# Another hand-fixed order of the same 573 steps in a two-part state-space kernel on one core

## The chip, the core and the metric

The kernel runs on one core of a Trainium2 chip. The metric is the device time of one execution in microseconds (us), lower is better. Five engines work side by side, each through its own instructions in a fixed order: PE (TensorE, matmuls), DVE (VectorE), ACT (ScalarE), POOL (GpSimd) and SP (SyncE, which here issues nearly all DMA transfers). [...] The time before is 198.16 us, the median of three runs (197.69 to 199.36).

## What is computed

Two independent parts, written side by side into one output of 2048 rows by 1280 columns.

```python
def _A_ref(x, Lambda_re, Lambda_im, B_re, B_im, C_re, C_im, log_dt, Dskip):   # S5
    Lam_bar = jnp.exp(dt * Lam)
    Bu = jnp.einsum("bld,pd->blp", x + 0j, B_bar)
    for t in range(L):
        h = Lam_bar[None, :] * h + Bu[:, t, :]
    y = 2.0 * jnp.einsum("blp,dp->bld", hseq, Cmat).real + x * Dskip[None, None, :]
...
def _B_ref(q, k, v, shift_k, ssm_k, ssm_D):                                    # H3
    k_shift = k_shift + k_pad[:, t:t + S, :] * shift_k[:, ks - 1 - t][None, None, :]
    kv = k_shift * v
    y = irfft(rfft(kv) * rfft(ssm_k))[:S]  +  kv * ssm_D
    return q * y
...
return jnp.concatenate([a, b], axis=-1)     # L = S = 2048, D = P = 640, 4 taps
```

The second part is cut here to its steps: the transform runs over the 2048 rows, zero-padded to 4096, per column.

## The kernel before, in words

Both parts are cut into five pieces of 128 columns: j = 0..4 for the states of part A, G = 0..4 for the columns of part B. `make_plan` (from line 737) declares 573 named steps, each with its engine, a length, and the steps that it needs. A string of step names, `ORDER`, is then walked once from front to back (`with tc.manual_schedule()`), and every step is recorded on its engine at that place. So the string fixes, for each engine apart, the order of its instructions; nothing is reordered later. A name with `@0`, `@2`, `@4` or `@6` takes one of four tiles of PSUM (128 x 1024 float32 each, shown as ps_64 to ps_67), and a name with `!` goes to the other of its two possible engines (an eviction, say, to DVE rather than to ACT, in the function `copy`, lines 465 to 469).

A matmul step on PE fills one of the four PSUM tiles; a step on ACT or DVE (an *eviction*) empties it; the next PE step with the same tile waits for that. PE executes in order, so such a wait holds up everything behind it.

Part A, for each j:
- `v1_j, v2_j, v3_j, v0_j` (PE, `pe_in`, L522 to L525): the input projection and a short recurrence over four interleaved row phases; evicted by `ve1_j` ... `ve0_j`.
- `rs, sc, ra, rout` (DVE; L536, L537 and L541, then the scan L551, then L536, L537 and L541 again): rotate, scan, rotate back. `rout_j` gives the states of phase 0. Then `oa`, `od` (DVE, L563 to L571) spread them to phases 1, 2 and 3.
- `ca`, `cs` (ACT and DVE, L445 to L453): scale the output matrix C. Its real and imaginary halves come by the transposing DMAs `CT0` and `CT1` (L840). `nH` (DVE, L319) negates a transform table.
- `p i_s` (PE, `pe_proj`, L584 and L589), 16 blocks of 128 rows (i) of phase s: the output projection, 20 matmuls in two halves. Every p needs the states of all five j, so the first, `p0_0`, can't start before the last `rout` (that is `rout3`). Evicted by `yo` (ACT, or DVE in L603 where the skip term is added there), stored by `yd` (SP, L611). `p3_2` is split into halves a and b.

Part B, for each G, a chain:
- `kT, vT` (SP, L617): load k and v transposed. `kS` (L625 or L627): a shifted copy of k. `dS` (DVE, L638): the tap matrices.
- `tap` (PE, L650) and `kv` (DVE, L655): four-tap convolution times v. `kvo`, `kvs` (SP, L658 and L631): kv goes out to DRAM and back in another layout. `hs` (SP, L631) and `had` (DVE, L634): the long kernel in that layout.
- `s1h, s1k` (PE, L666), `s2h, s2k` (PE, L679): two stages of the transform of the long kernel (h) and of kv (k), each evicted by `s1he, s1ke, s2he, s2ke` (L469 on ACT, L467 on DVE). `ya, y` (DVE, L691 to L697): the complex product.
- `inv` (PE, L705 to L708), `zs` (evictions), `zt` (SP, transposing, L716), `fin` (PE, L724), `ob` (DVE, L729, times q, which `qi` loads, L719), `od_` (SP store, L734).

The matrix shapes on PE differ: `tap` and `s1` use 64*64 pieces of the array, `s2` 128*64, all the rest 128*128.

SP issues its transfers in the order of the string, too, and waits at each for the steps that it needs; a transfer that is early in the string goes ahead on the DMA queue.

The lines that walk the string, which both kernels share:

```python
    names = [n.partition("@") for n in ORDER.split()]
    with tc.manual_schedule():
        for n, _, slot in names:
            fn, K.alt = plan[n.rstrip("!")][3], n[-1] == "!"
            if slot:
                fn(K.bank(int(slot)))
            else:
                fn()
```

## Time and profile before

| | us |
|---|---|
| median of 3 runs | 198.16 |
| the profiled execution, its own time | 197.26 |
| span of its instructions | 195.48 |
| PE busy | 183.3 (94%) |
| DVE busy | 174.9 (89%) |
| ACT busy | 145.9 (75%) |
| TensorE clock granted | 0.998 of full |

The profiled execution took 197.26 us: 195.48 us from its first instruction to its last, and 1.78 us around them. It is 0.90 us under the median. All sums below are differences against its span and are then put on the median.

How to read the rows: in a timeline a row has the start in us from the span's start, the duration, the engine, the line of the kernel, the operation, what is written and read, and how many instructions are merged in it; brackets at the end give the idle time ahead of it on that engine and what ended it. A row of the waits has who waited for whom, the sum in us, how often, and the longest. A row of the windows has the stretch, its length, and for PE, PEld (weight loads), DVE, ACT and POOL the busy us with the number of instructions; then the granted clock, the DMA share and GB/s.

Two habits of these rows matter here. PE overlaps its matmuls, so what a PE step costs is the time from its first start to the start of the step behind it, not the sum of durations. DVE overlaps the end of one instruction with the start of the next, too: an eviction lasts 1.22 us, but the next instruction starts 1.13 to 1.14 us after it.

### The profile page before, as it was taken

To read this page: it belongs to the slowest core of one execution; us is meant where nothing else is said; L and a number is where in the kernel's file an instruction comes from. 1 tells how busy PE (TensorE), PEld (TensorE's weight loads), DVE (VectorE), ACT (ScalarE), POOL (GpSimd) and SP (SyncE) were. 2 spreads that over 40 slices of the span, in tenths; PEclk is the share of its full clock that TensorE was granted. 3 is DMA by queue.
4 is the path that set the end of the run, shared out by engine and by line. 5 is a ranking of instruction groups with operands and counts; after the bars stand their busy time and mean duration, and the time that the engine had idled before them with its cause. 6 is when DMAs were issued, how large, how long until landed. Compare 5 with 4: busy or idle time off the path is not lost.

```text
span 195.5 us, 7462 instructions
## 1 busy us (share of the span) xinstructions
PE 183.3 (94%) x3304; PEld 125.5 (64%) x3304; DVE 174.9 (89%) x302; ACT 145.9 (75%) x179; POOL 24.7 (13%) x55
## 2 busy tenths in 40 slices
PE   7799999999999999999988889999899999999991
PEld 4444365544565455785668666888688877977770
DVE  5899877999999999998999999999888989899571
ACT  2499999976978898899989997798768874710100
POOL 8899562000000000000000000000000000000000
PEclk9999999999999999999999999999999999999999
DMA  4999999999999919869599999997991999198763
GB/s 119 199 223 195 179 216 207 195 212 169 195 207 149 163 22 257 172 95 172 160 161 124 182 176 231 192 170 163 166 223 38 188 157 326 32 199 186 212 170 104
DMA packets 126061, 33.75 MB, mean 173 GB/s; under 512 B 121032, under 2 KB 125389, under 8 KB 126029
## 3 DMA queue, kind: packets, MB, share of 16 engines
q1 hardware_dynamic: 125988, 33.27, 89.5%
q8 instruction: 26, 0.43, 0.9%
q14 instruction: 7, 0.05, 0.1%
q10 hardware_dynamic: 40, 0.01, 0.0%
HBM read 10.66 MB, written 7.86 MB: 95 GB/s over the span
## 4 chain that ended last, share of the span: by engine, by line
PE 65%; DVE 14%; ACT 13%; issue 3%; DMA 2%; POOL 0%; ACTq 0%; DVEq 0%; POOLq 0%
PE ps L584 23%; PE ps L522 13%; PE ps L679 6%; PE ps L666 4%; DMA h_st<-in_B_ssm_k_dram 2%; ACT Xs L469 2%; ACT kS L625 2%; ACT zz L469 2%; PE ps L705 2%; PE ps L524 2%; ACT As_h L469 2%; ACT Hf L469 2%; PE ps L525 2%; PE ps L708 2%; PE ps L706 2%
## 5 line engine op out<-in xcount | busy, mean ns | idle before, releaser
L522 PE MATMUL ps<-xT,BT 128*128 128x512 bf16 x200 | 48.5, 379 | 1.3 <-DMA xT<-in_A_x_dram 1.2
L584 PE MATMUL ps<-Cs,hs 128*128 128x320 bf16 x240 | 35.9, 299 | 0.7 <-issue 0.5
L522 PEld LDWEIGHTS <-BT 128*128 128x128 bf16 x200 | 18.7, 98 | 23.5 <-issue 1.5
L584 PEld LDWEIGHTS <-hs 128*128 128x128 bf16 x240 | 22.3, 98 | 8.9 <-issue 0.9
L469 ACT CAST BT<-ps 128x640 bf16<-128x640 f32 (+3 forms) x13 | 9.4, 726 | 17.9 <-PE ps L589 17.9
L679 PEld LDWEIGHTS <-G 128*64 128x64 bf16 x640 | 18.9, 110 | 4.4 <-issue 3.1
L469 ACT CAST As_h<-ps 128x1024 bf16<-128x1024 f32 x20 | 20.0, 1036 | 2.1 <-PE ps L666 2.1
L469 ACT CAST Hf<-ps 128x1024 bf16<-128x1024 f32 x20 | 20.0, 1028 | 1.4 <-PE ps L679 1.4
L469 ACT CAST As_kv<-ps 128x1024 bf16<-128x1024 f32 x19 | 18.8, 1023 | 2.4 <-PE ps L666 2.4
L469 ACT CAST Xs<-ps 128x1024 bf16<-128x1024 f32 x19 | 19.3, 1039 | 1.0 <-PE ps L679 1.0
L469 ACT CAST zz<-ps 128x1024 bf16<-128x1024 f32 x18 | 17.9, 1031 | 1.3 <-PE ps L708 1.0
L705 PE MATMUL ps<-Xs,H 128*128 128x128 bf16 x80 | 17.6, 220 | 0.0
L708 PE MATMUL ps<-Xs,H 128*128 128x128 bf16 x80 | 17.5, 219 | 0.0
L706 PE MATMUL ps<-Xs,H 128*128 128x128 bf16 x80 | 17.5, 219 | 0.0
L707 PE MATMUL ps<-Xs,H 128*128 128x128 bf16 x80 | 17.5, 219 | 0.0
L729 DVE TENSOR_TENSOR qb<-ps,qb 128x1024 bf16<-128x1024 f32 x10 | 12.1, 1222 | 3.6 <-PE ps L724 3.3
L691 DVE TENSOR_TENSOR rot<-Xs,Hf 128x2048 bf16<-128x2048 bf16 x10 | 12.2, 1222 | 1.2 <-ACT Xs L469 0.6
L697 DVE TENSOR_TENSOR Xs<-Xs,rot 128x1024 bf16<-128x1024 bf16 x20 | 12.9, 686 | 0.2
L655 DVE TENSOR_TENSOR vT<-ps,vT 128x1024 bf16<-128x1024 f32 x10 | 11.8, 1217 | 1.1 <-ACT h L469 0.7
L692 DVE TENSOR_TENSOR Xs<-Xs,Hf 128x2048 bf16<-128x2048 bf16 x10 | 12.2, 1225 | 0.5
L679 PE MATMUL ps<-As_kv,G 128*64 128x128 bf16 x320 | 11.9, 220 | 0.6 <-DVE vT L655 0.4
L679 PE MATMUL ps<-As_h,G 128*64 128x128 bf16 x320 | 11.6, 221 | 0.1
(205 smaller groups left out, 391.5 us busy)
## 6 DMA issues: line engine op xcount, KB each, us to landing
h_st<-in_B_ssm_k_dram SPq DMA_DIRECT2D x10, 256.0 KB, 4.4
kv_rows<-vT SPq DMA_DIRECT2D x5, 512.0 KB
qb<-in_B_q_dram SPq DMA_DIRECT2D x5, 512.0 KB
kv_st<-kv_rows SPq DMA_DIRECT2D x10, 256.0 KB, 4.7
out_dram<-qb SPq DMA_DIRECT2D x5, 512.0 KB, 5.0
out_dram<-BT SPq DMA_DIRECT2D x15, 160.0 KB, 3.2
BT<-in_A_x_dram SPq DMA_DIRECT2D x6, 160.0 KB, 4.5
As_kv<-in_A_B_re_dram SPq DMA_DIRECT2D x3, 160.0 KB, 2.3
```

What stands on the lines that cost most here:

```text
L469: self.nc.scalar.copy(out=out, in_=in_)
L522: mm(o, lhsT=self.BT[:, r, k, j * 128:(j + 1) * 128], rhs=xT[:, k, :], start=(k == 0), stop=(s == 1 and k == NT - 1))
L584: mm(o[:, 0:320], lhsT=h[:, r, ts], rhs=self.Cs[:, r, j, c0:c0 + 320], start=(j == 0 and r == 0), stop=(not on_pe and j == NT - 1 and r == 1))
L679: self.nc.tensor.matmul(o[64 * e:64 * e + 64, c:c + 128], lhsT=self.G[:, r, k, :], rhs=As[:, k, :], start=True, stop=True)
L691: tt(out=self.cross(), in0=X[:, ::-1, :], in1=self.Hf[:, 1:2, hs].to_broadcast([128, 2, 1024]), op=ALU.mult)
L692: tt(out=X, in0=X, in1=self.Hf[:, 0:1, hs].to_broadcast([128, 2, 1024]), op=ALU.mult)
L697: self.nc.vector.tensor_tensor(out=X[:, r, :], in0=X[:, r, :], in1=cr[:, r, :], op=ALU.add if r else ALU.subtract)
L705: mm(o_re, lhsT=self.H[:, 0, k1, :], rhs=yre, start=True, stop=False)
L706: mm(o_re, lhsT=self.H[:, 2, k1, :], rhs=yim, start=False, stop=True)
L707: mm(o_im, lhsT=self.H[:, 1, k1, :], rhs=yre, start=True, stop=False)
L708: mm(o_im, lhsT=self.H[:, 0, k1, :], rhs=yim, start=False, stop=True)
L729: self.nc.vector.tensor_tensor(out=self.qb[:, :, cs].rearrange("p a (i c) -> p a i c", c=4), in0=ps[:].rearrange("p a n -> p (a n)").rearr ...
```

## The change

The string `ORDER` is replaced from its second line on; in the first lines of that only tile numbers differ. No step is added or taken away, and `make_plan` stays as it is; so each engine's work is the same but for the evictions that change engine: `zs3_0, s1ke0_2, ve3_2, ve0_4, yo3_2b, zs0_3, s2ke1_3` lose their `!` (they go from DVE to ACT), and `s2he3_3, s2he1_2, s1ke1_3, s2he0_3, bge0, s2ke0_3` get one (they go from ACT to DVE). Until the step `v0_1` all engines do the same steps in the same order. Two lines of the diff, the first piece that stands in another order and its counterpart:

```diff
--- before.py
+++ after.py
@@ -941,38 +941,37 @@
...
-kv0_1@4 bge2@0 hp3 H2 dS1 hs0 kvo0 bg3@2 H3 ve0_0!@6 kT1 v0_1@0 rs0 bge3@2 ca0 sc0 bg0@4 ve0_1@0 v1_3@6 bge0@4 ve1_3@6 had0
-s1h0_2@2 s1he0_2@2 s1h0_0@0 s1he0_0@0 qi0 ra0 rout0 rs1 sc1 ra1 rout1 kS1 kvs0 v1_2@4 ve1_2@4 oa2_0 v1_4@6 s1h0_3@2 s1h0_1@0
...
+kv0_1@2 bge2@0 hp3 H2 dS1 hs0 kvo0 bg3@4 H3 ve0_0!@6 kT1 v0_1@0 rs0 bge3@4 ca0 sc0 bg0@2 ve0_1@0 v1_3@6 G2 CT1 had0 s1h0_0@4
+s1h0_2@0 ve1_3@6 bge0!@2 v1_4@2 s1he0_0@4 s1he0_2@0 ve1_4@2 vT1 kS1 ra0 nH rout0 oa2_0 od2_0 s1h0_1@6 tap1_1@4 s1h0_3@0 tap1_0@2
...
```

What moves, at three places.

**SP's queue, from the second load of k (kT1) on.** Before: after kT1 come the load of q (qi0), the reload of kv (kvs0, two DMAs), v of the second piece (vT1), the imaginary half of C (CT1), and the kernel rows of G = 1 (hs1).

```order
L658 DMA kv_rows<-vT 128x2048
L617 DMA_TRANSPOSE kT<-in_B_k_dram 128x2048
L719 DMA qb<-in_B_q_dram 128x16x128
L631 DMA kv_st<-kv_rows 64x32x64 x2
L617 DMA_TRANSPOSE vT<-in_B_v_dram 128x2048
L840 DMA_TRANSPOSE Cs<-in_A_C_im_dram 128x5x640
L631 DMA h_st<-in_B_ssm_k_dram 64x32x64 x2
```

On the same queue now:

```order
L658 DMA kv_rows<-vT 128x2048
L617 DMA_TRANSPOSE kT<-in_B_k_dram 128x2048
L840 DMA_TRANSPOSE Cs<-in_A_C_im_dram 128x5x640
L617 DMA_TRANSPOSE vT<-in_B_v_dram 128x2048
L631 DMA kv_st<-kv_rows 64x32x64 x2
L631 DMA h_st<-in_B_ssm_k_dram 64x32x64 x2
L658 DMA kv_rows<-vT 128x2048
L617 DMA_TRANSPOSE kT<-in_B_k_dram 128x2048
L719 DMA qb<-in_B_q_dram 128x16x128
```

CT1 has moved ahead of vT1 and kvs0, and qi0 has moved behind the next kvo and kT.

**DVE, from the first scan on.** Before, the row of L551 is the scan of j = 0 (sc0), then had0, ra0, rout0 (hs_140 is phase 0 of j = 0), then rs1 to rout1 of j = 1, then kS1 and oa2_0:

```order
L551 SCALAR_TENSOR_TENSOR z_150<-rr_88,rot 128x512 x2
L634 TENSOR_TENSOR h_st<-h_st,dcol_b 128x32
L536 TENSOR_TENSOR rot<-tabs,z_150 128x1024
L537 TENSOR_TENSOR rot<-tabs,z_150 128x1024
L541 TENSOR_TENSOR hs_140<-rot 128x512 x2
L536 TENSOR_TENSOR rot<-tabs,z_151 128x1024
L537 TENSOR_TENSOR rot<-tabs,z_151 128x1024
L541 TENSOR_TENSOR rot<-rot 128x512 x2
L551 SCALAR_TENSOR_TENSOR z_151<-rr_88,rot 128x512 x2
```

The same place now (the piece ends with dS2, the two kv of G = 1 follow):

```order
L551 SCALAR_TENSOR_TENSOR z_150<-rr_88,rot 128x512 x2
L634 TENSOR_TENSOR h_st<-h_st,dcol_b 128x32
L467 CAST BT<-ps_65 128x2x4x128
L627 COPY kS<-kT 64x1032 x2
L536 TENSOR_TENSOR rot<-tabs,z_150 128x1024
L537 TENSOR_TENSOR rot<-tabs,z_150 128x1024
L319 TENSOR_SCALAR H<-H 128x2048
L541 TENSOR_TENSOR hs_140<-rot 128x512 x2
L563 TENSOR_SCALAR rot<-hs_140,lam 128x1024
L564 TENSOR_SCALAR rot<-hs_140,lam 128x512
L565 TENSOR_SCALAR rot<-hs_140,lam 128x512
L570 TENSOR_TENSOR rot<-rot,hs_140 128x1024
```

The scan of j = 1 has moved back behind part B's kS1, nH, kv1_0, kv1_1 and cs0; the eviction bge0 (BT<-ps_65) stands on DVE ahead of kS1.

**The end, on SP.** Before, the last stores: the other half of p3_2, the store of part B, and three full blocks; the last block, p1_1, goes through DVE.

```order
L611 DMA out_dram<-BT 128x320
L611 DMA out_dram<-BT 128x640 x2
L611 DMA out_dram<-BT 128x320
L734 DMA out_dram<-qb 128x16x128
L611 DMA out_dram<-BT 128x640 x3
```

And now:

```order
L611 DMA out_dram<-BT 128x640
L611 DMA out_dram<-BT 128x320
L611 DMA out_dram<-BT 128x640
L734 DMA out_dram<-qb 128x16x128
L611 DMA out_dram<-BT 128x640 x3
L611 DMA out_dram<-BT 128x320
```

The last block is now p3_2b, a half, evicted by ACT, and part B's last transforms on PE, fin4_0 and fin4_1, stand together ahead of the last three projection steps p1_1, p2_1 and p3_2b; before, p2_1 stood between them, and p3_1 and p1_1 came last.

## The prediction

> **What bounds the kernel now.** I read the page's busy shares, then the windows, since no one engine is full over the whole span, then the waits of DVE and PE in the windows, and last the timelines where one window hands over to the next.

> ```profile
> PE 183.3 (94%) x3304; PEld 125.5 (64%) x3304; DVE 174.9 (89%) x302; ACT 145.9 (75%) x179; POOL 24.7 (13%) x55
> ```

> PE looks like the bound, with 12 us of idle time. The windows say where.

> ```profile
> 34.86:113.93 79.07, 75.90 (x1672) 48.13 (x1673) 76.76 (x112) 70.57 (x78) 0.00 (x0) 1.00 0.94 165
> 113.93:142.00 28.07, 26.10 (x715) 21.32 (x711) 26.55 (x39) 23.76 (x28) 0.00 (x0) 1.00 1.04 181
> 142.00:191.40 49.40, 49.38 (x723) 39.37 (x721) 41.91 (x69) 23.24 (x27) 0.00 (x0) 1.00 0.79 175
> 191.40:195.50 4.10, 0.00 (x0) 0.00 (x0) 0.82 (x1) 0.00 (x0) 0.00 (x0) 0.93 0.20 69
> ```

> The first window runs from the first rotation (rs0) to the end of rout3, the last state that the projections need. DVE is busy 76.76 of its 79.07 us. All its waits over 0.15 us there are one:

> ```profile
> DVE vT L655 <- ACT h L469: 0.7, 1, 0.7
> ```

> The other 1.6 us are steps of 0.03 to 0.1 us between dependent instructions. So DVE sets the pace from 34.86 to 113.93, and PE's gaps there cost nothing by themselves. From 142 PE is busy 49.38 of 49.40 us: it sets the end. The hand-over is the first projection block p0_0. The rows of DVE around rout3 (L541), then those of PE around p0_0:

> ```profile
> 113.18 0.75 DVE L541 TENSOR_TENSOR hs<-rot 128x512 bf16<-128x512 bf16 x2
> 113.84 1.22 DVE L655 TENSOR_TENSOR vT<-ps,vT 128x1024 bf16<-128x1024 f32 x1
> 114.98 1.22 DVE L691 TENSOR_TENSOR rot<-Xs,Hf 128x2048 bf16<-128x2048 bf16 x1
> ```

> ```profile
> 115.91 1.52 PE L584 MATMUL ps<-Cs,hs 128*128 128x320 bf16 x10 [0.21 <-ACT As_h L469]
> ...
> 118.45 1.11 PE L584 MATMUL ps<-Cs,hs 128*128 128x320 bf16 x7 [0.48 <-issue]
> ```

> p0_0 starts at 115.91, 1.98 us after rout3 is done, since PE first waits for evictions of part B. From there to PE's end at 191.4 (the window's end) are 75.5 us, nearly all work. PE's waits in that stretch:

> ```profile
> PE ps L666 <- issue: 0.5, 1, 0.5
> PE ps L584 <- issue: 0.5, 1, 0.5
> PE ps L679 <- ACT zz L469: 0.3, 1, 0.3
> ```

> The two called issue stand inside one step, where nothing is waited for by a semaphore; their cause isn't shown, and I leave both in the new order. So the end is the sum of three stretches: up to p0_0, from p0_0 to PE's end, and the tail of 4.1 us.

> **Term 1: the start of p0_0.** Ahead of rout3 DVE has the same work but for three edits. Five evictions leave DVE (s1ke0_2, ve3_2, ve0_4, zs0_3, s2ke1_3) and five come (bge0, s2he0_3, s2ke0_3, s1ke1_3, s2he1_2): nothing, ACT being 70.57 busy of 79.07 and so the cover. The pair oa3_1, od3_1 is replaced by oa3_0, od3_0: nothing. And kv4_0 (the L655 row behind rout3) now stands ahead of it: 114.98 - 113.84 = +1.14 us. Without any wait rout3 would end at 113.93 - 0.70 + 1.14 = 114.37. To this come new waits, and the place to look is where the string now asks for data early. The DVE rows that price the way there:

> ```profile
> 39.23 0.69 DVE L536 TENSOR_TENSOR rot<-tabs,z 128x1024 bf16<-128x1024 bf16 x1
> ...
> 41.42 0.69 DVE L536 TENSOR_TENSOR rot<-tabs,z 128x1024 bf16<-128x1024 bf16 x1
> ...
> 47.92 0.88 DVE L627 COPY kS<-kT 64x1032 bf16<-64x1032 bf16 x2
> ...
> 52.22 2.35 DVE L655 TENSOR_TENSOR vT<-ps,vT 128x1024 bf16<-128x1024 f32 x2
> ...
> 54.48 0.68 DVE L638 TENSOR_TENSOR diagS<-id,sk_b 128x512 bf16<-128x512 bf16 x1
> ...
> 55.68 1.22 DVE L467 CAST h<-ps 128x1024 bf16<-128x1024 f32 x1
> ```

> had0 ends its slot at 39.23, bge0 takes 1.14, so kS1 is asked for at 40.4 (before at 47.92). Behind it ra0 and rout0 (41.42 - 39.23 = 2.19), kS1, oa2_0 and od2_0 (52.22 - 47.92 less one eviction of 1.14 = 3.16), dS2 and nH (55.68 - 54.48 = 1.20): kv1_0 is asked for at 40.4 + 6.55 = 46.95 (the pair of kv started at 52.22). kS1 needs the load kT1, kv1_0 needs vT1. SP's rows, the first vT and then the stretch in question, and the rows of issues (KB each, median us to landing) and of packets:

> ```profile
> 13.24 2.88 SPq L617 DMA_TRANSPOSE vT<-in_B_v_dram  x1
> ```

> ```profile
> 34.27 4.39 SPq L617 DMA_TRANSPOSE kT<-in_B_k_dram  x1
> 38.77 0.52 SPq L719 DMA_DIRECT2D qb<-in_B_q_dram  x1
> 39.38 4.06 SPq L631 DMA_DIRECT2D kv_st<-kv_rows  x2
> 43.48 3.62 SPq L617 DMA_TRANSPOSE vT<-in_B_v_dram  x1
> 47.15 4.27 SPq L840 DMA_TRANSPOSE Cs<-in_A_C_im_dram  x1
> ```

> ```profile
> DMA packets 126061, 33.75 MB, mean 173 GB/s; under 512 B 121032, under 2 KB 125389, under 8 KB 126029
> ...
> kv_st<-kv_rows SPq DMA_DIRECT2D x10, 256.0 KB, 4.7
> ...
> vT<-in_B_v_dram SPq DMA_TRANSPOSE x5, 5.0
> kT<-in_B_k_dram SPq DMA_TRANSPOSE x5, 4.5
> ...
> Cs<-in_A_C_im_dram SPq DMA_TRANSPOSE x1, 7.8
> ```

> [...] The load of C lands 7.8 us after its issue began, 3.5 after it ended; a vT 5.0 after. kT1's issue ends at 38.66 in both orders; with 2.1 us behind it (an estimate: a vT's 5.0 less the 2.88 us of the first one's issue) it lands at 40.8, with 3.5 us at 42.2: kS1 waits 0.4 to 1.8 us. I take 0.7, near the lower end, because a kT has 4.5, the shortest of the three.

> vT1 now has CT1 ahead of it, and no longer qi0 and kvs0. By issue times that is 38.66 + 4.27 + 3.62 + gaps of 0.15 = 46.7 at its end, landing at 48.8 to 50.2. By bytes at 173 GB/s, 0.82 MB (640 x 640 x 2) take 4.7 us and 2 x 0.52 MB 6.0 us, so that its end comes 1.3 us earlier than the 47.10 of before, at 45.8, and the landing at 47.9 or later. The lower end for kv1_0 is no wait beyond kS1's. I take a landing at 48.2, near the byte sum, since issue times hide what still waits in the queue: kv1_0 starts 1.2 us late in all (0.4 to 3.2).

> [...]

> Behind kv1_0 stand cs0 (CT1 comes 8 us earlier than before), rs1, had1 and cs1. They move with it, and so do the PE steps that wait for the tiles that kv frees. kvs0 comes later by CT1 and vT1 less qi0 (4.7 + 3.0 - 3.0 us); s1k0_2, its first user, comes later too, behind v2_4 at some 53 us. Its issue ended at 43.44 before; 4.7 us later, with 4.7 us to landing, it is there at 52.8 at the latest, so I cost it at nothing, with little to spare. I add one more wait of 0.4 us: ya1_0 now stands right behind kv3_0, while its last eviction, s2he1_1, is queued on ACT behind kS3 and three other evictions (0 to 0.7 us, the size of the one wait that DVE has now). rout3 then ends at 114.37 + 1.2 + 0.4 = 115.97. PE has s1h3_3 directly ahead of p0_0, which needs the tile that kv4_0 frees, done before rout3; so p0_0 follows rout3 at once, at 116.0 instead of 115.91: **+0.1 us** (114.8 to 118.5).

> **Term 2: from p0_0 to PE's end.** The work is the same. What differs is how often PE changes its array shape. Two projection blocks, one followed by 128*128 work, one by 128*64 work:

> ```profile
> 163.20 1.52 PE L584 MATMUL ps<-Cs,h 128*128 128x320 bf16 x10
> ...
> 166.20 0.57 PE L724 MATMUL ps<-Mq,zz 128*128 128x64 bf16 x14
> ```

> ```profile
> 132.65 1.52 PE L584 MATMUL ps<-Cs,hs 128*128 128x320 bf16 x10
> ...
> 135.74 0.64 PE L679 MATMUL ps<-As_kv,G 128*64 128x128 bf16 x16
> ```

> 166.20 - 163.20 = 3.00 against 135.74 - 132.65 = 3.09: a change of shape costs 0.09 to 0.10 us. Counted along the string, PE changes shape 23 times behind p0_0 before and 18 times now (s2h3 and s2k3 stand in fours, fin1 and inv2 in one piece): 5 x 0.1 = -0.5 us. The wait of 0.3 us (s2k3_2 for a tile that zs2_1 frees) goes, because s2k3_1 now stands behind four inv2 steps: -0.3. Late next are the DVE steps. p0_2 now needs od2_4, which ends some 18 us behind rout3 by the starts of its steps, where PE gets to p0_2 some 20 us behind p0_0's start; p0_1 needs od1_0, about even. I cost these at nothing (0 to +1). **-0.8 us.**

> **Term 3: the tail.** Before, p1_1 is evicted by DVE and stored as one full block; now a half block, p3_2b, by ACT.

> ```profile
> 191.42 0.82 DVE L603 TENSOR_TENSOR BT<-ps,BT 128x640 bf16<-128x640 f32 x1 [1.53 <-PE ps L584]
> 192.28 0.33 SPq L611 DMA_DIRECT2D out_dram<-BT  x1
> ```

> ```profile
> L469 ACT CAST BT<-ps 128x320 bf16<-128x320 f32 x1 | 0.4, 426 | 4.6 <-PE ps L589 4.6
> ```

> ```profile
> out_dram<-BT SPq DMA_DIRECT2D x15, 160.0 KB, 3.2
> ...
> out_dram<-BT SPq DMA_DIRECT2D x2, 80.0 KB, 2.2
> ```

> The eviction is shorter by 0.82 - 0.43 = 0.39. The store has 80 KB less, 0.47 us at 173 GB/s, or 1.0 by the medians. I take the bytes, because the last store finds an idle queue: **-0.8 us** (-0.4 to -1.4). yd2_1, the full store ahead of it, is issued a p3_2b (1.5 us) earlier and so ends no later.

> **Sum**: 0.1 - 0.8 - 0.8 = -1.5 us. On the profiled execution 195.48 - 1.5 = 194.0 span; on the median 198.16 - 1.5 = **196.7 us**. Its own range, from the middle part of each term: 195.6 to 197.9.

> **Rivals.**
> 1. *The loads hide and PE doesn't stumble.* kS1 waits 0.4, kv1_0 no longer, ya1_0 not: p0_0 at 114.37 + 0.4, that is -1.1; the two issue gaps fall elsewhere, -1.0; with terms 2 and 3 it is -3.7: 194.5. For it: the gaps have no cause in the kernel. Against: ACT and PE don't run ahead of DVE by much.
> 2. *The early loads come late.* vT1 lands at 50.2, kv1_0 is 3.2 us late: p0_0 at 118.0, +2.1; the sum is +0.5: 198.7, no change. For it: SP's issues of over 4 us; against: qi0 has left that part.
> 3. *DVE and PE wait for each other* (slower). In the new order DVE evicts s2he0_3, s2ke0_3, s1ke1_3 and s2he1_2 and frees eight tiles by kv between 47 and 114 us, and PE stands behind it each time; when PE is then late, DVE waits for PE and ACT at its next step. Each such turn costs what the one does now, 0.7 us. Two turns bring it back to 198.1; from five on (+3.5) the kernel is slower: 200.2. For it: PE has no step to fall back on in a fixed order. Against: before, five evictions of the same kind cost DVE one such wait.
> 4. *Nothing to gain.* DVE's busy time is the same in both orders, and what PE saves is waited out elsewhere: 198.2. [...]

> **How the numbers follow.** The forecast has a chance of 0.42, rival 1 0.18, rival 2 0.15, rival 3 0.18, rival 4 0.07. A measurement of this kernel can tell about 1% from no change, so faster means under 196.2 and slower over 200.1. Faster: rival 1 and a third of the forecast, 0.18 + 0.14 = 0.32. Slower: two thirds of rival 3 and the far end of rival 2, 0.12 + 0.04 = 0.16. Same: 0.52. For 8 in 10 the range goes from rival 1's price, 194.5, to just short of rival 3's, 200.0, and leaves out about half of each, 0.18.

> **What the new profile would show.** Term 1: kS1 (the first 64-partition copy behind the first scan) at 41.1 and the first kv of G = 1 at 48.2, DVE busy to within 3 us from 34.86 to rout3, rout3's end at 116.0 and p0_0 right behind. Rival 1 has p0_0 before 115, rival 2 a DVE wait of over 2 us on a DMA ahead of a kv, rival 3 many DVE waits for PE between 50 and 114 and p0_0 after 118. Term 2: 74.7 us from p0_0 to PE's end, with no wait on an eviction over 0.3 us. Term 3: 3.3 us from PE's end to the span's end. The prediction is wrong if DVE waits more than 3 us in all ahead of rout3, or if PE waits for DVE behind p0_0.

## The result, and the profile after

The new order takes 196.4 us (median of 20 runs, 195.61 to 197.84) where the old one takes 198.06 (20 runs, 197.09 to 199.37): a ratio of 0.9933, with a 95% interval of 0.9914 to 0.9953. The forecast was 196.7. The gain is 1.66 us between the medians and 1.3 us (0.9 to 1.7) by the ratio; by the bounds that the prediction set for "same" (196.2 to 200.1) it counts as no change, though the interval keeps clear of 1.

The two profiled executions don't show this difference. That of the new order took 197.57 us, one of its longer ones; that of the old order took 197.26, one of its shorter ones. So I took another profile of the new order and two more of the old one (`after_again`, `before_again`, `before_third`; labels of runs stand like this from here on). The table cuts each span at the start of p0_0 and at PE's end, as the prediction did; the points are read from the timelines, the lengths from the windows that follow.

| profile | time us | p0_0 starts | p0_0 to PE's end | tail | span |
|---|---|---|---|---|---|
| before | 197.26 | 115.91 | 75.47 | 4.1 | 195.5 |
| before_again | 197.4 | 116.14 | 75.36 | 4.1 | 195.6 |
| before_third | 197.98 | 116.15 | 75.84 | 4.1 | 196.1 |
| after | 197.57 | 116.70 | 75.57 | 3.5 | 195.8 |
| after_again | 197.26 | 116.37 | 75.57 | 3.6 | 195.5 |

Windows of the new order, cut at rs0, the end of rout3, 142 us, PE's end and the end (columns: length, busy time and instructions of PE, weight loads, DVE, ACT and POOL, granted clock, DMA share, GB/s):

```profile
35.11:116.40 81.29, 76.90 (x1772) 49.39 (x1781) 77.90 (x112) 72.39 (x79) 0.00 (x0) 1.00 0.97 172
116.40:142.00 25.60, 24.18 (x614) 19.74 (x605) 23.64 (x37) 21.55 (x26) 0.00 (x0) 1.00 0.99 173
142.00:192.27 50.27, 50.02 (x726) 39.74 (x715) 43.42 (x71) 23.59 (x28) 0.00 (x0) 1.00 0.74 169
192.27:195.80 3.53, 0.00 (x1) 0.00 (x0) 0.00 (x0) 0.43 (x1) 0.00 (x0) 1.00 0.21 71
```

The same windows of `before_third`, whose time of 197.98 us is close to the old order's median:

```profile
35.12:114.17 79.05, 75.93 (x1672) 48.15 (x1672) 76.76 (x112) 70.51 (x78) 0.00 (x0) 1.00 0.92 161
114.17:142.00 27.83, 26.05 (x715) 21.27 (x712) 26.44 (x40) 23.71 (x28) 0.00 (x0) 1.00 0.99 176
142.00:191.99 49.99, 49.73 (x724) 39.50 (x721) 41.95 (x69) 23.41 (x27) 0.00 (x0) 1.00 0.78 173
191.99:196.10 4.11, 0.00 (x0) 0.00 (x0) 0.82 (x1) 0.00 (x0) 0.00 (x0) 0.77 0.20 69
```

DVE has 77.90 - 76.76 = 1.14 us more work ahead of rout3's end: kv4_0, as forecast. The tail is 0.58 us shorter. But DVE is idle 3.39 us in its first window where it was idle 2.29. Its waits there in `after`:

```profile
DVE kS L627 <- DMA kT<-in_B_k_dram: 1.5, 1, 1.5
DVE z L467 <- PE ps L525: 1.0, 1, 1.0
DVE As_kv L467 <- issue: 0.3, 1, 0.3
DVE vT L655 <- PE ps L650: 0.3, 1, 0.3
```

The wait of 1.0 stands ahead of rs0, outside the window. The one of 1.5 is kS1 waiting for kT1. In `after_again` that wait is another:

```profile
DVE vT L655 <- DMA vT<-in_B_v_dram: 0.7, 1, 0.7
DVE As_kv L467 <- issue: 0.4, 1, 0.4
DVE kS L627 <- DMA kT<-in_B_k_dram: 0.3, 1, 0.3
```

So the waits for the two early loads are 1.5 us in one execution and 1.0 in the other, and differently shared. From p0_0 on, the first row of p0_0 on PE and then the rows of `after` with a stall (an idle time inside a step that ends with "issue"):

```profile
116.70 1.52 PE L584 MATMUL ps<-Cs,hs 128*128 128x320 bf16 x10 [0.21 <-ACT As_kv L469]
...
119.30 0.99 PE L584 MATMUL ps<-Cs,hs 128*128 128x320 bf16 x6 [0.40 <-issue]
...
124.95 0.31 PE L589 MATMUL ps<-diagD,xT 128*128 128x64 bf16 x3 [0.62 <-issue]
```

p0_0 stalls as before (0.48 in the first profile of the old order), and now p1_0 stalls too, where the old order stalled in s1k4_0 (0.51).

### The profile page after: what moved, and what is told of

It reads as the page before. It is cut to its first block, busy times and chain, and to the rows that moved or that the text cites. A ratio compares the mean times of both kernels' runs of the same rounds, so it can differ in the third digit from the quotient of the medians.

```text
span 195.8 us, 7439 instructions
## 1 busy us (share of the span) xinstructions
PE 183.5 (94%) x3289; PEld 125.8 (64%) x3304; DVE 173.8 (89%) x301; ACT 146.4 (75%) x180; POOL 24.8 (13%) x55
## 2 busy tenths in 40 slices
DMA packets 126060, 33.75 MB, mean 172 GB/s; under 512 B 121031, under 2 KB 125388, under 8 KB 126028
## 4 chain that ended last, share of the span: by engine, by line
PE 57%; DVE 19%; ACT 14%; issue 4%; DMA 4%; POOL 0%; DVEq 0%; ACTq 0%; POOLq 0%
PE ps L584 19%; PE ps L522 12%; PE ps L679 5%; ACT Xs L469 4%; DMA kT<-in_B_k_dram 4%; PE ps L666 3%; PE ps L524 3%; PE ps L525 2%; ACT Hf L469 2%; DVE qb L729 2%; DVE H L388 2%; ACT As_h L469 2%; PE ps L325 1%; ACT zz L469 1%; PE ps L724 1%
## 5 line engine op out<-in xcount | busy, mean ns | idle before, releaser
L522 PE MATMUL ps<-xT,BT 128*128 128x512 bf16 x185 | 47.7, 379 | 1.8 <-DMA xT<-in_A_x_dram 0.8
L584 PE MATMUL ps<-Cs,hs 128*128 128x320 bf16 x240 | 35.7, 299 | 0.7 <-issue 0.4
L469 ACT CAST BT<-ps 128x640 bf16<-128x640 f32 (+3 forms) x13 | 8.8, 682 | 27.3 <-PE ps L589 26.7
L584 PEld LDWEIGHTS <-hs 128*128 128x128 bf16 x240 | 22.3, 98 | 9.1 <-issue 0.9
L679 PEld LDWEIGHTS <-G 128*64 128x64 bf16 x640 | 18.8, 110 | 6.0 <-issue 5.1
L469 ACT CAST zz<-ps 128x1024 bf16<-128x1024 f32 x20 | 19.6, 1035 | 1.5 <-PE ps L708 1.5
L469 ACT CAST As_h<-ps 128x1024 bf16<-128x1024 f32 x20 | 20.1, 1028 | 0.7 <-PE ps L666 0.6
L469 ACT CAST As_kv<-ps 128x1024 bf16<-128x1024 f32 x19 | 19.0, 1025 | 0.6 <-PE ps L666 0.6
L469 ACT CAST Hf<-ps 128x1024 bf16<-128x1024 f32 x17 | 17.1, 1021 | 2.7 <-PE ps L679 2.6
L469 ACT CAST Xs<-ps 128x1024 bf16<-128x1024 f32 x19 | 18.7, 1040 | 0.4 <-PE ps L679 0.4
L691 DVE TENSOR_TENSOR rot<-Xs,Hf 128x2048 bf16<-128x2048 bf16 x10 | 12.2, 1224 | 0.6
L679 PE MATMUL ps<-As_h,G 128*64 128x128 bf16 x320 | 11.4, 220 | 1.3 <-DVE vT L655 1.3
L655 DVE TENSOR_TENSOR vT<-ps,vT 128x1024 bf16<-128x1024 f32 x10 | 11.8, 1218 | 0.7 <-PE ps L650 0.7
L551 DVE TENSOR_TENSOR_SCAN z<-rr,rot 128x512 bf16<-128x512 f32 x10 | 11.7, 1209 | 0.0
## 6 DMA issues: line engine op xcount, KB each, us to landing
h_st<-in_B_ssm_k_dram SPq DMA_DIRECT2D x10, 256.0 KB, 5.1
kv_st<-kv_rows SPq DMA_DIRECT2D x10, 256.0 KB, 4.2
```

The source lines that it names most:

```text
L469: self.nc.scalar.copy(out=out, in_=in_)
L522: mm(o, lhsT=self.BT[:, r, k, j * 128:(j + 1) * 128], rhs=xT[:, k, :], start=(k == 0), stop=(s == 1 and k == NT - 1))
L584: mm(o[:, 0:320], lhsT=h[:, r, ts], rhs=self.Cs[:, r, j, c0:c0 + 320], start=(j == 0 and r == 0), stop=(not on_pe and j == NT - 1 and r == 1))
L679: self.nc.tensor.matmul(o[64 * e:64 * e + 64, c:c + 128], lhsT=self.G[:, r, k, :], rhs=As[:, k, :], start=True, stop=True)
L691: tt(out=self.cross(), in0=X[:, ::-1, :], in1=self.Hf[:, 1:2, hs].to_broadcast([128, 2, 1024]), op=ALU.mult)
```

## The experiments

Twelve runs: three repeat a kernel for another profile, nine are variants. The variants move names in the string and nothing else. In a diff, a `+` stands for the variant, a `-` for the new order unless said otherwise.

**A second profile of the new order.** No edit.

> The new order once more, beside the others on the same chip. Both theories: 0.993 of the time before. Its profile is a second look at the same instructions: where its span differs from the first profile's 195.8 us, the stretch that differs is what varies from execution to execution. Theory: the length of the stretch from p0_0 to PE's end stays within 0.3 us of 75.6 but for the gaps inside a step on PE; the start of p0_0 varies with kS1's wait for the load kT1 (1.5 us in the first profile).

Measured: 196.53 us, a ratio of 0.9936 (0.9908 to 0.9964). From p0_0 to PE's end it takes 75.57 us, as in the first profile, and p0_0 starts 0.33 us earlier. So what varies here lies ahead of p0_0.

**The last block.** A full block that DVE evicts comes last again.

```diff
-p1_1@2 p2_1@6 xd2_1 yo1_1@2 xd3_1 yo3_1@0 yo2_1@6 yd1_1 yd3_1 yd2_1 p3_2b@4 yo3_2b@4 yd3_2b
+p1_1@2 p3_2b@4 yo3_2b@4 p2_1@6 xd2_1 yo1_1@2 xd3_1 yo3_1@0 yo2_1@6 yd1_1 yd3_1 yd3_2b yd2_1
```

> The new order, but the half block p3_2b stands ahead of p2_1 on PE, so a full block that DVE evicts is last again. It undoes the third term alone. Theory: 0.4 to 0.8 us above the new order, ratio to before 0.995 to 0.997; the stretch from PE's end to the span's end 4.0 to 4.2 us instead of 3.5. Rival (the last store is hidden behind others anyway): same as the new order, 0.993.

Measured: 197.05 us, a ratio of 0.9984 (0.9966 to 1.0003). Against the 0.9936 of the new order on the same chip that is 0.48% of 198 us, about 0.9 us, with wide intervals; between the medians (196.53 and 197.05) it is 0.52 us. The ratio lies above the 0.995 to 0.997 that I expected. Its windows from rs0 to rout3, from p0_0 to PE's end and behind that, and then its waits of DVE up to rout3:

```profile
35.12:115.12 80.00, 77.45 (x1784) 49.29 (x1781) 77.96 (x112) 72.28 (x79) 0.00 (x0) 1.00 0.93 167
115.44:191.03 75.59, 74.11 (x1308) 59.31 (x1307) 66.03 (x105) 45.27 (x52) 0.00 (x0) 1.00 0.83 171
191.03:195.10 4.07, 0.00 (x1) 0.00 (x0) 0.82 (x1) 0.00 (x0) 0.00 (x0) 1.00 0.13 45
```

```profile
DVE z L467 <- PE ps L525: 1.0, 1, 1.0
DVE As_kv L467 <- issue: 0.3, 1, 0.3
DVE vT L655 <- PE ps L650: 0.3, 1, 0.3
```

The tail is 4.07 us again, where the new order's two profiles have 3.53 and 3.56: 0.53 us by the trace, which is the exacter figure and is what I expected. The second reading matters more: this kernel has the new order's head unchanged, and in this execution DVE waits for neither kT1 nor vT1. p0_0 starts at 115.44. So the waits for the early loads come and go from one execution to the next.

SP's rows say where they come from. SP begins the issue of kT1 at 34.93 us in `after`, at 33.81 in `after_again` and at 32.71 in `full_last`, behind the same transfers in the same order, while DVE is ready for kS1 at 40.7 in all three. The transposing loads at the start had taken SP longer in the first two: the three of x and kT0 together 14.0 and 13.1 us, against 11.8 in `full_last`. `head_only` and `head_clean`, where kT1's issue begins at 32.7 too, have no such wait either. Why those first loads take longer in some executions isn't shown.

**The two halves, joined at p0_0.** `head_only` has the new order up to p0_0 and the old one behind it, `rest_only` the other way round. The heads differ by one s1 step of PE and its eviction, and by a pair oa, od, so each seam has a run of steps that neither kernel has:

```diff
 head_only, against the new order
 s1ke3_2@6 s1he3_0@0 s1ke3_0@4 s1he3_3@2
-p0_0@6 s1k3_1@0 s1h3_2@4 s1k3_3@2
+oa3_1 od3_1 s1h3_2@4 s1he3_2@4 p0_0@2 od_0 zt1_1 zt1_0
 rest_only, against the old order
 s1he3_3@6 s1ke3_0@0 s1he3_2@4
-p0_0@2 od_0 zt1_1 zt1_0
+oa3_0 od3_0 s1k3_2@6 s1ke3_2@6 p0_0@6 s1k3_1@0 s1k3_3@2
```

> The new order up to p0_0, behind it the old order of what is left (four steps differ between the two heads). Theory of three terms: the head gains nothing (+0.1 forecast, +0.8 in the first profile), the rest is the old one, so the time is 198.1 to 198.9, ratio 1.000 to 1.004. Rival: the gain was made ahead of p0_0 (earlier states, fewer waits of DVE in a typical execution), then the ratio is 0.993.

> The old order up to p0_0, then the new order of what is left. Theory of three terms: -0.8 us from p0_0 to PE's end and -0.8 us of tail, ratio 0.992. Rival (the gain is in the head): 1.000. If the new rest only fits a DVE that is as far as in the new head, PE waits for DVE's od steps at p0_2 or p3_3 and part of the 1.6 us is lost: 0.995.

Measured: 201.36 us (1.0224, 1.0183 to 1.0266) and 201.5 us (1.0218, 1.0193 to 1.0243). Both halves slower than either whole says that the cut itself costs. PE's rows at the seam of `head_only`, then its windows of 2 us:

```profile
117.46 0.32 PE L666 MATMUL ps<-R,h_st 64*64 64x64 bf16 x17 [2.04 <-ACT As_kv L469]
...
118.48 2.51 PE L584 MATMUL ps<-Cs,hs 128*128 128x320 bf16 x10
```

```profile
116.00:118.00 2.00, 0.32 (x17) 0.21 (x16) 1.86 (x5) 2.00 (x3) 0.00 (x0) 1.00 1.36 99
118.00:120.00 2.00, 1.76 (x23) 1.14 (x24) 1.97 (x2) 1.34 (x2) 0.00 (x0) 0.72 1.07 344
120.00:122.00 2.00, 2.00 (x11) 1.31 (x10) 1.93 (x4) 0.00 (x0) 0.00 (x0) 0.50 1.37 227
122.00:124.00 2.00, 2.00 (x46) 1.40 (x45) 1.97 (x2) 0.64 (x2) 0.00 (x0) 0.93 0.43 63
```

s1h3_2 waits 2.04 us for its tile, PE is then busy 0.32 us of two, and the granted clock falls to 0.50: ten matmuls of p0_0 take 2.51 us, not 1.52. `rest_only` has a wait of 1.1 us and a stall of 1.8 at its seam, and the clock at 0.50 from 118 to 124 us. Neither run tells the halves apart.

**The two halves, joined where they agree.** Just behind rout3 both orders have done the same steps, but for one pair oa, od that can be exchanged. Behind the seam the tiles are renamed so that no step takes one that has just been filled.

```diff
 rout3 s2k2_2@4 s2ke2_2@4 s1h3_0@0
-s1k3_2@6 s1k3_0@4 s1h3_3@2 s1ke3_2@6 s1he3_0@0 s1ke3_0@4 s1he3_3@2 p0_0@6 s1k3_1@0 s1h3_2@4
+s1he3_0@0 s1k3_0@6 s1h3_3@2 s1h3_2@4 s1he3_3@2 s1ke3_0@6 s1he3_2@4 p0_0@0 od_0 zt1_1
```

That is `head_clean`; `rest_clean` joins the old head to the new rest at the same place.

> The new order up to s1h3_0, just behind rout3, then the old order; the seam is put where both orders have done the same steps but for one pair oa, od, and the tiles behind it are renamed so that PE doesn't wait at it. Theory A (only the tail gains): a ratio of 1.000, 0.998 to 1.002. Theory B (the head gains 0.7 to 1 us): 0.995 to 0.9965. Either way the granted clock stays at 1.00 around the seam and PE waits less than 0.5 us there; if it is 0.5 there again, the first seam's idle time was not what lowered it.

> The old order up to s1he3_1, just behind rout3, then the new order with its tail. Theory A: all of the gain is here, a ratio of 0.993 to 0.9955. Theory B: the tail's 0.55 us and no more, 0.9965 to 0.998. The profile should have 75.5 to 75.7 us from p0_0 to the end of PE and 3.55 us behind it, and no stretch at half clock.

Measured: 198.28 us (1.0021, 0.9995 to 1.0047) and 196.59 us (0.993, 0.9911 to 0.9949). The clock stays at 1.00. The ratios are those of theory A, by which only the tail gains, but the traces show that neither theory holds. `rest_clean` from p0_0 to PE's end, with its p0_0 and p1_0:

```profile
117.17:191.38 74.21, 73.77 (x1308) 59.55 (x1307) 65.25 (x105) 43.94 (x50) 0.00 (x0) 1.00 0.83 176
191.38:194.90 3.52, 0.00 (x0) 0.00 (x0) 0.00 (x0) 0.43 (x1) 0.00 (x0) 0.86 0.21 70
```

```profile
117.17 1.52 PE L584 MATMUL ps<-Cs,hs 128*128 128x320 bf16 x10 [0.62 <-ACT As_kv L469]
...
118.67 1.52 PE L584 MATMUL ps<-Cs,hs 128*128 128x320 bf16 x10
...
121.20 1.53 PE L584 MATMUL ps<-Cs,hs 128*128 128x320 bf16 x10
...
122.71 1.52 PE L584 MATMUL ps<-Cs,hs 128*128 128x320 bf16 x10
```

p0_0 comes 1.0 us later than in `before_again`, and the rest takes 74.2 us rather than 75.4 to 75.8, because PE doesn't stall once. The profiled execution of `head_clean`, the longest of its twelve (200.17 us), is the opposite. PE's waits from 74 us on, of 0.3 us and more:

```profile
PE ps L679 <- issue: 1.1, 2, 0.6
PE ps L708 <- issue: 1.0, 1, 1.0
PE ps L584 <- issue: 0.7, 1, 0.7
PE ps L666 <- issue: 0.6, 2, 0.4
...
PE ps L707 <- issue: 0.4, 1, 0.4
...
PE ps L724 <- issue: 0.3, 1, 0.3
```

Stalls of 4.1 us in all, spread over eight places. So the halves don't add up: what one order does changes where the other stalls, and the stalls had to be explained first.

**Two more profiles of the old order.** No edit.

> The kernel before, unchanged, for a second profile of it. In its first profile p0_0 starts at 115.91, and PE takes 75.5 us from there to its end, as in every profile of the new order (75.6); the tail is 0.55 us shorter in the new one. Theory A, the tail is the whole gain: this profile shows p0_0 at 115.9 again, to within 0.3 us, and a span of 195.3 to 195.8. Theory B, the first profile of before was one of its quick executions, and the new order also gains some 0.7 to 1 us ahead of p0_0: p0_0 at 116.4 or later, a span of 196 or more, and the 75.5 us behind p0_0 the same.

> The kernel before, unchanged, for a third profile. The two so far have spans of 195.5 and 195.6, quicker than its median execution (a time of 198.0 is a span of 196.2), and p0_0 at 115.9 and 116.1. If what varies is PE's stalls inside steps (0.3 to 0.8 us each, at places 128 weight loads apart), this profile has the same work and waits, and differs from the other two only in which of the places stall. If it is DVE's waits for loads, they show ahead of rout3 (over 0.3 us, where both profiles had none on a DMA).

Measured: 197.4 and 197.98 us, spans of 195.6 and 196.1. Up to p0_0 they agree to 0.01 us (116.14, 116.15) and show no wait for a load; both start rs0 0.25 us later than the first profile. They differ in the stalls: `before_again` has none in p0_0, 0.34 us in s1k4_0 and 0.42 in s1h4_1; `before_third` has 0.28, 0.52 and 0.26. p0_0 comes 0.24 us later than in the first profile. By the margins that I gave, `before_again` fits theory A (115.9 to within 0.3 us, a span of 195.3 to 195.8) and not theory B (116.4 or later). But theory A's conclusion, that the tail is the whole gain, doesn't follow from it: what was out of the usual was the late p0_0 of the new order's two profiles, which `full_last` doesn't have. So what varies in the old order is the startup, a little, and the stalls; no wait for a load shows.

**The load kT1 ahead of kvo0.** SP issues it one transfer earlier.

```diff
-H2 dS1 hs0 kvo0 bg3@4 H3 ve0_0!@6 kT1 v0_1@0 rs0
+H2 dS1 hs0 kT1 kvo0 bg3@4 H3 ve0_0!@6 v0_1@0 rs0
```

> The new order with one load moved: SP issues the load kT1 ahead of kvo0 rather than behind it, so that kS1 finds its data. In the profile of the new order DVE waits 1.5 us for it. If DVE sets the pace up to rout3, as the first window says, most of that passes to the end: rout3 and p0_0 1.0 to 1.5 us earlier (p0_0 near 115.2), a ratio of 0.986 to 0.989. If the wait is only passed on (to the next step that waits for a load, or to PE and ACT): p0_0 as in the new order and 0.993. If what is issued later is what counts (kvo0 and what stands behind it): 0.995 or more.

Measured: 196.42 us, 0.9922 (0.9899 to 0.9946), no further than the new order's 0.9933 and 0.9936. Its windows, cut as those of `full_last`:

```profile
35.09:115.10 80.01, 76.90 (x1772) 49.34 (x1782) 77.98 (x112) 72.37 (x79) 0.00 (x0) 1.00 0.96 170
115.34:190.93 75.59, 74.11 (x1308) 59.39 (x1307) 66.92 (x106) 44.85 (x51) 0.00 (x0) 1.00 0.83 170
190.93:194.50 3.57, 0.00 (x0) 0.00 (x0) 0.00 (x0) 0.42 (x1) 0.00 (x0) 0.82 0.22 74
```

The wait for kT1 is gone and p0_0 comes at 115.34, as I expected, but the median stays. The expectation of 0.986 to 0.989 was a miss: it took the 1.5 us of one profile for the usual case. Together with `full_last` this suggests that most executions of the new order don't have that wait.

**What PE's stalls are.** The places are fixed: counted in weight loads from the start, every stall of 0.2 us and more from rs0 on, in all 14 profiles, stands at 1119, 1502, 1630, 2013, 2141, 2525, 2653 or 2781, multiples of 128 apart to within 2, whichever step stands there; no execution stalls at all of them. 128 weight loads with their matmuls are 256 instructions, and the instruction queue carries 26 packets of 16 KB, one for each 128 of the 3304 pairs. The queues in `after` (packets, MB, share of the 16 engines):

```profile
q1 hardware_dynamic: 125988, 33.27, 89.4%
q8 instruction: 26, 0.43, 0.9%
```

From the trace, for the last packet ahead of such a place:

```
kernel        place  step    packet starts  ends     next weight load   behind the end   stall
before        2013   p0_0    116.09         117.02   118.45             1.44             0.48
before        2525   s1k4_0  138.61         139.48   141.07             1.59             0.51
after         2013   p0_0    116.98         117.91   119.30             1.39             0.40
after         2141   p1_0    122.33         123.65   124.94             1.29             0.62
kt_early      2141   p1_0    120.96         122.10   123.60             1.50             0.62
rest_clean    2013   p0_0    116.55         117.47   119.08             1.61             none
q_late        2141   p1_0    123.66         125.03   127.40             2.36             none
zt_late       2141   p1_0    119.94         121.14   122.47             1.33             none
loads_spread  2141   p1_0    120.10         121.17   123.00             1.83             none
```

A PE that stalls goes on 1.2 to 1.6 us after the packet has ended. Nor does PE pass such a place sooner where it doesn't stall: at all these places of the 14 profiles (counted to within two loads) the next weight load starts 1.25 us or more behind the packet's end. So by these times a stall is PE waiting for its packet, though no record in the trace names that wait; in p0_0 and p1_0 the packet is late. The next two kernels ask why.

**Loads out of the packets' way.** Both start from kT1 early and change SP's order alone; the diffs show only SP's steps.

```diff
 q_late
-zt1_1 zt1_0 kvo4 qi1 hs4
+zt1_1 zt1_0 kvo4 hs4 qi1
 zt_late
-od_0 zt1_1 zt1_0 kvo4 qi1
+od_0 kvo4 zt1_0 zt1_1 qi1
```

> The kernel with kT1 early, and one more move on SP's queue: the load qi1 behind hs4 rather than ahead of it. PE, DVE and ACT have the same instructions in the same order. In p1_0 PE stalls 0.6 us at a weight load 128 behind the one where it stalls in p0_0; a 16 KB packet of the instruction queue starts 2.9 us ahead of it, where it starts over 3.1 us ahead at the places that don't stall. Theory C, the packet is late because the queues are still full of kvo4's, zt1's and qi1's bytes: with qi1 out of the way the packet starts earlier, p1_0 takes 3.1 to 3.4 us and not 3.9, and the ratio goes from 0.992 to 0.988 to 0.990. Theory D, the stall has nothing to do with the loads: p1_0 stays at 3.9 and the ratio at 0.992. If qi1 comes too late for ob1_0, DVE waits there for a DMA and 0.992 or more.

> The kernel with kT1 early, and the two transposes zt1 behind kvo4 rather than ahead of it; PE, DVE and ACT are the same. The stretch from 109 to 115 us then has no transposes in the queues. Theory C: the packet for p0_0's place starts earlier than 2.8 us ahead of it, and p0_0 takes 3.1 us and not 3.68; p1_0 stalls as before or worse, since the transposes now run ahead of its place; the ratio 0.989 to 0.991. Theory D: p0_0 and p1_0 unchanged, the ratio 0.992. fin1_0, which needs zt1_0, isn't late by more than 0.5 us (the transpose is issued by 119 and fin1_0 starts at 125.8).

Measured: 198.13 us (1.0012, 0.9985 to 1.0038) and 197.4 us (0.9986, 0.9958 to 1.0013). The stalls that theory C said would go went. In `q_late` the packet for p1_0 starts 3.6 us ahead of the place, where it was 1.6 with kT1 early, and p1_0 takes 3.10 us and not 3.90. In `zt_late`, where the transposes are out of the way, the packet for p0_0 starts 2.6 us ahead, not 1.4, and p0_0 takes 3.09 us, not 3.68:

```profile
115.57 1.52 PE L584 MATMUL ps<-Cs,hs 128*128 128x320 bf16 x10 [0.21 <-ACT As_kv L469]
...
117.07 1.53 PE L584 MATMUL ps<-Cs,hs 128*128 128x320 bf16 x10
```

But theory C also said that p1_0 would stall in `zt_late` as before or worse, and there it takes 3.10 us without a stall, though the transposes are being issued (115.41 to 122.03) while its packet is fetched. So that moving the loads moves the stalls is shown; which loads hold up which packet, and how, is not. Nor does the start of the packet decide it alone, as the 2.9 and 3.1 us of my expectation would have it: in `rest_clean` and in `loads_spread`, the last kernel below, p0_0's packet starts 2.4 us ahead of the place, but it takes 0.92 us in the one and 1.53 in the other, and only in the second does p0_0 lose time (0.2 us).

On the time I was wrong, but for the case that I had named for `q_late`: qi1 now lands too late for ob1_0. DVE's waits behind 118 us in `zt_late`, and then those of `q_late` behind 118 us and ahead of it:

```profile
DVE qb L729 <- DMA qb<-in_B_q_dram: 2.0, 1, 2.0
```

```profile
DVE qb L729 <- DMA qb<-in_B_q_dram: 2.1, 1, 2.1
```

```profile
DVE vT L655 <- DMA vT<-in_B_v_dram: 2.5, 1, 2.5
```

The last is the wait of the prediction's rival 2, kv1_0 for vT1, in a long execution (202.18 us against a median of 198.13), in which p0_0 starts 4 us later than usual; its p1_0 is weaker evidence for that reason. PE waited 2.31 us behind it, and its clock was at 0.53 from 52 to 54 us.

**Loads where they hinder least.** qi1 goes right behind the store that frees its buffer, the transposes behind kvo4, and yd0_0 (late in `zt_late`, where PE waited 1.1 us for a tile that hung on it) ahead of hs4. SP's steps again, against kT1 early.

```diff
-od_0 zt1_1 zt1_0 kvo4 qi1 hs4 kvs4 yd0_0
+od_0 qi1 kvo4 zt1_0 zt1_1 yd0_0 hs4 kvs4
```

> The kernel with kT1 early, and SP's queue around p0_0 arranged so that no step waits for its load and the queues hold little when PE's packets are due: qi1 right behind od_0, then kvo4, the two transposes zt1, yd0_0, and only then hs4 and kvs4. PE, DVE and ACT are the same. Theory C (PE's stalls in p0_0 and p1_0 come from packets that wait behind other bytes, and what zt_late and q_late lost was qi1 coming late for ob1_0, 2.0 us, and yd0_0 late for yo2_0, 1.1 us): p0_0 at 115.4, 3.1 to 3.4 us long, p1_0 3.1, no wait of DVE on qb, 74.2 to 74.6 us from p0_0 to PE's end, a span of 193.2 to 193.9 and a ratio of 0.985 to 0.988. Rival: the bytes cost the same wherever they stand; a stall or a wait of a step on a load comes up elsewhere, and the ratio is that of kT1 early, 0.991 to 0.994. If hs4 or kvs4 come too late for the next rank's s1 steps at 143: 0.995 or more.

Measured: 195.93 us (195.09 to 196.35), a ratio of 0.9904 (0.9875 to 0.9933), the best of all here and faster than the old order. From the new order (0.9914 to 0.9953) the intervals don't part it. Its windows:

```profile
35.11:115.30 80.19, 76.54 (x1749) 49.04 (x1761) 78.08 (x112) 72.19 (x79) 0.00 (x0) 1.00 0.92 166
115.89:190.45 74.56, 74.14 (x1308) 59.66 (x1307) 66.58 (x106) 44.83 (x51) 0.00 (x0) 1.00 0.86 174
190.45:194.00 3.55, 0.00 (x1) 0.00 (x0) 0.00 (x0) 0.42 (x1) 0.00 (x0) 1.00 0.22 74
```

The ratio that theory C gave, 0.985 to 0.988, was missed. The rest takes 74.56 us rather than 75.59, as theory C has it: p0_0 3.3 us, p1_0 3.1, and no wait for q. But p0_0 starts at 115.89, not 115.4, since a stall of 0.6 us ahead of rout3 (in inv1_3, place 1630) and a wait of 0.3 us of PE for a store came up there; half of the 1.0 us is given back.

## Why the prediction was right in sum, and not in its parts

The sum: -1.5 us forecast, -1.66 measured between the medians. For the parts I take executions near the medians: `before_third` for the old order, and for the new one the head of `full_last` (no wait for a load) with the 75.57 and 3.55 us of its own profiles: 115.44 + 75.57 + 3.55 = 194.6, which is the span of the new order's median (196.4 less 1.77, the difference of time and span). That the usual execution is put together like this is worked out, not seen in one profile. Nor do the halves joined behind rout3 show the split between terms 1 and 2: by their medians all of the gain goes with the new rest (196.59 us; the new head with the old rest takes 198.28), and the stalls, which fall differently in each, cover what the head alone does. The tail is shown, by `full_last`; the -0.7 and -0.3 below stay argued.

| term | forecast | usual executions | the two first profiles |
|---|---|---|---|
| 1, start of p0_0 | +0.1 | 115.44 - 116.15 = -0.7 | +0.8 |
| 2, p0_0 to PE's end | -0.8 | 75.57 - 75.84 = -0.3 | +0.1 |
| 3, tail | -0.8 | 3.55 - 4.11 = -0.6 | -0.6 |
| sum | -1.5 | -1.6 | +0.3 |

So that the sum came out is luck: term 1 came out 0.8 us below its forecast, and terms 2 and 3 together 0.7 us above theirs.

**Term 1** had the right mechanism and a wrong size. kv4_0's 1.14 us came as forecast (DVE busy 77.96 us against 76.76 in its window). Without any wait for a load, rout3 ends at 115.12 with rs0 at 35.12; moved to the first profile's start of 34.86 that is 114.86, against 114.37 + 0.4 = 114.77 by the prediction's rows. That these agree so well is partly chance: the wait of 0.4 us that I put on ya1_0 doesn't show, and the two of 0.3 us that do stand elsewhere (a kv behind PE's tap, and an eviction with "issue", whose cause the trace doesn't give). And PE follows 0.3 us behind, not 2 us as in the old order. The step that failed is the price of the early loads: I put 1.2 us on them; they cost 1.5 us in `after`, 1.0 in `after_again`, and nothing in `full_last`, `head_only` and `head_clean`, which issue the two loads in the same places. I took the end of kT1's issue in the first profile of the old order, 38.66 us, as given for both orders, and there SP was late, as in `after` (39.19). In `before_again` and `before_third` that issue ends at 35.96 and 36.19, in `full_last` at 35.50; with the 2.1 to 3.5 us that I put behind it, kT1 is there ahead of 40.4. (With kT1 early, `q_late` had 2.5 us for vT1 and the three others none.) So the lower ends that I gave, 0.4 and no wait, were nearest to the usual case, and rival 1 was right on this point.

The forecast's other error here hid the first: the start of 115.91 that I compared with was that of a quick execution; the other two profiles of the old order have 116.14 and 116.15.

**Term 2** failed. Between the first two profiles the stretch grew by 0.1 us. I sum up what each step takes above the shortest such step in five profiles (both orders, `before_third`, `kt_early`, `rest_clean`), from its first matmul to the next step's, and take off 0.1 us from a wait where the shape changes too:

```
                                  before   after
stalls inside steps               1.34     1.37    p0_0 0.64, s1k4_0 0.70 | p0_0 0.57, p1_0 0.80
waits for a tile, ahead of        0.61     1.03    s2k3_2 0.35, inv2_2 0.18, p2_2 0.08 | s2k4_0 0.41, inv2_0 0.22, p2_0 0.20, inv3_3 0.20
changes of shape, and the rest    2.44     2.09
sum                               4.39     4.49
```

The wait ahead of s2k3_2 went, as forecast, but others came that I hadn't costed: 0.41 us ahead of s2k4_0, which needs the tile that ob2_0 frees, and three of 0.2 us, so that waits cost 0.42 more and not 0.3 less. The fewer changes of shape (18, not 23, as counted) together with the rest brought 0.35 us and not 0.5. The price of a change held, as a projection block in `after` takes 3.00 us ahead of 128*128 work and 3.09 to 3.10 ahead of another shape; where the other 0.15 us went isn't shown. That is rival 4's mechanism, what PE saves is waited out, within this stretch. The wait ahead of s2k4_0 is also a sign by which I had said that the prediction would be wrong, PE waiting for DVE behind p0_0 (ob2_0 is a DVE step). In the view of the waits it is 0.2 us, since PE overlaps its matmuls (the 16 ahead of it last 0.22 us each and are done in 0.64):

```profile
PE ps L679 <- DVE qb L729: 0.2, 1, 0.2
```

The other sign, waits of DVE of more than 3 us ahead of rout3, didn't come: they are 2.1 us in `after`. The stalls I left in with no known cause, and their sum stayed the same only by accident: 1.37 us is lost to them in the new order, more than the whole term, and `rest_clean` shows the stretch without them at 74.2.

**Term 3** had the right sign and mechanism: -0.55 us by the trace where I took -0.8. The eviction was 0.43 us as forecast (-0.39); what was oversized is the store, 0.16 us shorter for its 80 KB less and not 0.47. The row of it in `after`:

```profile
192.31 0.43 ACT L469 CAST BT<-ps 128x320 bf16<-128x320 f32 x1 [9.56 <-PE ps L589]
```

**Rival 3** (DVE and PE wait for each other ahead of rout3) didn't occur in the new order: from rs0 to rout3, DVE waits for PE once, for 0.3 us, in both of its profiles. Where PE is held up otherwise, by stalls in `head_clean` or by the late vT1 in `q_late`, such waits do appear, 1.4 and 1.6 us of them.

## What to carry to other kernels

One profile is one execution: when the expected change is 1%, take two or three profiles of both kernels before putting a price on a wait for a load, since here the same wait was 0, 0.3 and 1.5 us. Idle time inside a step that ends with "issue" deserves a cause before it is carried over: here it was PE's own instruction packets, which came late while loads were under way, and moving a load, two transposes and a store brought 1 us on that stretch (75.59 us in `kt_early`, 74.56 in `loads_spread`). When an order is cut in two to find which half gains, join the halves where both have done the same steps, or the seam is what is measured.
